# Token transforms of a spectral filter, split by even and odd frequency into quarters and halves of the TensorE array

## The chip, the cores and the metric

The kernel runs on one core of one Trainium2 chip. The metric is the time of one execution on the device in microseconds (us). Before the change the median of three runs is 439.57 us (439.55 to 439.62). One further execution was recorded by the profiler; durations, starts and waits below come from it.

## The reference, cut to what matters

```
xn  = layernorm(x)                                    # x: 2048 tokens x 448 channels
A   = irfft2(rfft2(xn) * (w_r + 1j * w_i))            # over tokens and channels, 225 channel frequencies
B   = (relu(xn @ W_gate) * (xn @ W_up)) @ W_down      # 448 -> 1792 -> 448
out = x + A + B
```

Everything is float32. The kernel writes each operand as a sum of two float16 parts, a high one and a low one, and multiplies high by high, high by low and low by high: three TensorE passes stand for one float32 product.

## The kernel before, in words

**Two streams of work share the engines.** The foreground is the gated network B: 56 gate units (14 slices of the hidden width times 4 chunks of tokens), each 40 passes of 512 columns on TensorE (some of them half passes over 64 rows), and three groups of down projections. After a gate unit ScalarE takes the relu (`gu_relu`, L966), VectorE multiplies by the up half (`gu_times`, L970, called the gate product below), ScalarE writes the high part (`gu_hi`, L974) and VectorE the low part (`gu_lo`, L978). Two PSUM buffers `gu` hold gate units, so the next but one unit can start when the gate product has read its buffer.

The background is the spectral branch A. A token number is 16 n1 + n2 and a token frequency is k1 + 128 k2. So the forward transform is, for each of 16 values n2, a channel transform (`f_dft`, for the pair n2 and n2 + 8), an eight-point butterfly on VectorE (`f_a`, `f_b`), the two float16 parts (`f_hi`, `f_lo`) and a transform over 128 tokens n1 (`f_sdft`), then a sixteen-point butterfly over n2. The spectrum is multiplied by the filter, and the inverse goes back the same way: `i_join` (last butterfly), `i_swap` (DMAs that bring cosine and sine rows to each other's partitions), `i_pair` (their sum), `i_mix` (an eight-point butterfly in two halves), `i_hi` on ScalarE and `i_lo` on VectorE, the token transform `i_sdft`, its two float16 parts `i_pqhi` (ScalarE) and `i_pqlo` (VectorE), and the channel transform `i_ddft`, which adds into the output. The inverse goes through p = 0 to 7, each p standing for the pair p and p + 8.

In `f_sdft` the stationary operand is a 128x128 matrix of cosines and sines and the moving one has 464 columns: three passes for each n2. In `i_sdft` the data stand still and the matrix moves: four blocks of 128, three passes of 128 columns each. Both use the whole array. `f_dft` and `i_ddft` use its two halves of 64 rows side by side. Their results and those of the token transforms go to two PSUM banks named `fx`.

**What sets the order.** The foreground units are emitted in a fixed sequence. Behind each, a planner takes background steps off a list. Each step carries a cost in VectorE time, and a share `load` of a unit's time, found by bisection, says how much background fits behind a unit, so that the list ends nine gate units before the end. A scheduler then puts the instructions into a fixed order for each engine; an engine takes its own in that order and waits on semaphores. `f_dft` and `i_ddft` are "offered": if half passes of a gate unit come by they are placed behind these, and every later matmul that is emitted is tied behind them (`state["bar"]`).

Of the kernel before, what the change touches and what calls it, by code (L numbers as in the profile page):

```python
# [20 lines left out]
NG = 8  # L21
# [23 lines left out]
SQ = 2.0 ** -16  # L45

# [29 lines left out]

def _freqs():


    p = np.arange(128)  # L80
    k1 = np.where(p < 64, p, np.where(p == 64, 64, 64 - p))
    return (k1[None, :] + 128 * np.arange(16)[:, None]) % S


def _constants():
# [54 lines left out]
    c_fm = c_fm.reshape(4, 4, 128, 2, 128).transpose(1, 2, 0, 3, 4)  # L140
# [6 lines left out]
def tile_gfnet_reglu(ctx: ExitStack, tc: tile.TileContext, x, xr, wgu, wd, wf, ident, c_fd, c_fm, c_im, c_row, c_id,  # L147
# [35 lines left out]

    eps = mt([128, 1], F32, "eps")
# [21 lines left out]
    state = {}  # L206
# [45 lines left out]
    def load_fm(q):  # L252
        t = ft([128, 4, 2, 128], F16, "fm", 4)
        nc.sync.dma_start(t, c_fm[q])
        for j in range(4):
            fm_t[q + 4 * j] = t[:, j]
# [155 lines left out]
    Fq, Xh, yps, cur = {}, {}, {}, {}  # L412
# [235 lines left out]
    def swap(key):  # L648
# [4 lines left out]
        nc.sync.dma_start(t[1:64], cur[key][65:128])  # L653
        nc.sync.dma_start(t[65:128], cur[key][1:64])
# [9 lines left out]
    def row_in(j):  # L664
        for par in range(2):
            nc.sync.dma_start(row[j + 8 * par:j + 8 * par + 1], cur["s1", j, par][64:65])

    def row_wf():
# [5 lines left out]
        for i in range(4):  # L674
            nc.sync.dma_start(w[32 * i:32 * i + 16], wf[:, 64, i // 2])
# [63 lines left out]
    def i_swap(p):  # L739
        u = U[p]  # L740
        for i in range(2):
            nc.sync.dma_start(u[64:65, :, :, KC * i:KC * (i + 1)], row[p + 8 * i:p + 8 * i + 1])
        t = sw[p] = state["sw"][p % 2]
        nc.sync.dma_start(t[1:64], u[65:128])
        nc.sync.dma_start(t[65:128], u[1:64])
# [26 lines left out]
    def i_sdft(n2):  # L772
        ps = fx()
        v, m = state["vt"][:, :, n2 // 8].rearrange("p a g k -> p a (g k)"), im_t[n2]
        for g in range(4):
            o = ps[:, 128 * g:128 * (g + 1)]
            for i, (h, c) in enumerate(((0, 0), (0, 1), (1, 0))):
                mm(o, v[:, h, 128 * g:128 * (g + 1)], m[:, c, :], start=(g + i == 0), stop=(i == 2),
                         skip_group_check=True)
        sps[n2] = ps  # L780

    def i_pqhi(n2):
        pgh[n2] = it([128, 1024], F16, "wf", 6).rearrange("p (a k) -> p a k", a=2)
        A.activation(pgh[n2][:, 0], sps[n2], AF.Copy, scale=2.0 ** -14)  # L784

    def i_pqlo(n2):
        V.scalar_tensor_tensor(pgh[n2][:, 1], sps[n2], 2.0 ** -14, pgh[n2][:, 0], op0=OP.mult, op1=OP.subtract)  # L787
# [259 lines left out]
    PE_US = {"f_dft": 0.85, "f_sdft": 0.59, "i_sdft": 0.65, "i_ddft": 0.82, "row_dft": 0.2}  # L1047
# [40 lines left out]
    add(0.0, f_dft, 0, 8)  # L1088
    for k, a in enumerate(seq):
# [14 lines left out]
        if k < 7:  # L1104
            add(0.0, force, f_dft, seq[k + 1], seq[k + 1] + 8)
        for n2 in (a, a + 8):
            add(0.0, f_sdft, n2)
# [84 lines left out]
    both(0.6, i_pqlo, 7)  # L1192
# [252 lines left out]
def _arrays(A_x, A_w_r, A_w_i, B_W_gate, B_W_up, B_W_down):  # L1445
# [39 lines left out]
```

## Time and profile before

| what | value |
|---|---|
| median of three runs | 439.57 us |
| profiled execution, first to last instruction | 438.4 us |
| TensorE (PE) busy | 430.9 us, 98% |
| VectorE (DVE) busy | 371.2 us, 85% |
| ScalarE (ACT) busy | 256.8 us, 59% |
| GpSimd (POOL) busy | 36.4 us, 8% |
| mean granted TensorE clock | 1.000 |

The profiled execution's own time is its span; no other time of it is given, and the median of the runs is 1.2 us above. A matmul's listed duration contains its way through the pipeline, so the pace of a block of matmuls is read from the starts of its first and of the next block. The same holds for VectorE, where the next instruction starts before the listed end of the last. "Idle before" in square brackets names what an engine waited for.

### The profile page before, as it was taken

The numbers are of one execution on the slowest core, as the hardware profiler recorded it, in microseconds if no ns is written. First come the engines' busy times: TensorE is split into PE (matmuls) and PEld (weight loads), VectorE is DVE, ScalarE is ACT, GpSimd is POOL, SyncE is SP. The second block draws the span as 40 slices with busy tenths as digits, with TensorE's granted clock in tenths as the row PEclk, the third lists the DMA queues.
The fourth block names the chain that finished last, engine by engine and source line by source line (L and its number), as shares of the span: only waits on it lengthen the run. The fifth ranks groups of instructions, "written<-read, shape, count | busy, mean of one in ns | idle before, by whom it ended". The sixth has DMA issues, their size and how long they took to land.

```text
span 438.4 us, 8109 instructions
## 1 busy us (share of the span) xinstructions
PE 430.9 (98%) x3014; PEld 209.9 (48%) x3014; DVE 371.2 (85%) x916; ACT 256.8 (59%) x519; POOL 36.4 (8%) x72
## 2 busy tenths in 40 slices
PE   6999999999999999999999999999999999999997
PEld 2644544454444444444444444444554555554544
DVE  5998798999967999899999999698989978976213
ACT  5897494486357856625413675574565665756620
POOL 1140040033300040000000011000000000000000
PEclk9999999999999999999999999999999999999999
DMA  8769992042000363530402100020111121301112
GB/s 261 253 164 304 384 236 65 2 80 31 3 0 2 133 198 119 163 120 24 144 13 86 43 1 1 2 81 7 55 45 53 47 67 56 119 24 50 43 42 84
DMA packets 37720, 39.53 MB, mean 90 GB/s; under 512 B 17952, under 2 KB 32576, under 8 KB 37680
## 3 DMA queue, kind: packets, MB, share of 16 engines
q1 hardware_dynamic: 37680, 39.01, 29.3%
q8 instruction: 23, 0.38, 0.4%
q14 instruction: 17, 0.14, 0.1%
HBM read 24.25 MB, written 3.67 MB: 64 GB/s over the span
## 4 chain that ended last, share of the span: by engine, by line
PE 97%; ACT 1%; DMA 1%; DVE 0%; issue 0%; SPq 0%
PE gu L450 59%; PE dn L450 27%; PE fx L450 7%; PE dn L1034 1%; PE gu L1034 1%; DMA y<-in_xr 1%; ACT tt L330 1%; ACT junk L192 0%; PE fx L406 0%; PE fx L1034 0%; ACT y L321 0%; DVE bst L265 0%; ACT rs L282 0%; PE gu L384 0%; DVE xy L1013 0%
## 5 line engine op out<-in xcount | busy, mean ns | idle before, releaser
L450 PE MATMUL gu<-T,wt 128*128 128x512 f16 (+2 forms) x1250 | 269.6, 376 | 0.0
L450 PEld LDWEIGHTS <-wt 128*128 128x128 f16 (+1 forms) x1250 | 111.7, 97 | 141.4 <-issue 19.9
L450 PE MATMUL dn<-wdt,h 128*128 128x448 f16 x624 | 126.8, 353 | 0.0
L450 PEld LDWEIGHTS <-h 128*128 128x128 f16 x624 | 60.2, 98 | 57.3 <-issue 0.4
L974 ACT ACTIVATE h<-g 128x512 f16<-128x512 f32 x56 | 35.1, 626 | 61.4 <-DVE g L970 61.3
L970 DVE SCALAR_TENSOR_TENSOR g<-gu,g 128x512 f32<-128x512 f32 x56 | 38.5, 687 | 21.0 <-ACT g L966 20.9
L966 ACT ACTIVATE g<-gu 128x512 f32<-128x512 f32 x56 | 33.0, 590 | 35.4 <-PE gu L450 35.4
L1006 ACT ACTIVATE xy<-dn,dsc 128x448 f32<-128x448 f32 x44 | 27.6, 627 | 28.0 <-PE dn L450 27.9
L978 DVE TENSOR_TENSOR h<-g,h 128x512 f16<-128x512 f32 x56 | 38.4, 687 | 5.5 <-ACT h L974 5.5
L995 ACT ACTIVATE dn<-xy,dinv 128x448 f32<-128x448 f32 x44 | 27.8, 632 | 0.6
L195 POOL PARTITION_ALL_REDUCE wm<-wm x15 | 13.8, 929 | 170.5 <-ACT junk L192 170.5
L866 DVE SCALAR_TENSOR_TENSOR wt<-wst,wsc,wt 128x512 f16<-128x512 f32 x28 | 20.4, 747 | 3.8 <-ACT wt L862 3.8
L862 ACT ACTIVATE wt<-wst,wsc 128x512 f16<-128x512 f32 x28 | 19.2, 715 | 1.0 <-DVE wsc L202 0.9
L787 DVE SCALAR_TENSOR_TENSOR wf<-fx,wf 128x512 f16<-128x512 f32 x16 | 10.8, 690 | 8.9 <-ACT wf L784 8.9
L192 ACT ACTIVATE junk<-wst 128x512 bf16<-128x512 f32 x28 | 17.4, 623 | 1.3 <-DMA wst<-in_wgu 1.1
L784 ACT ACTIVATE wf<-fx 128x512 f16<-128x512 f32 x16 | 9.5, 597 | 9.8 <-PE fx L450 9.2
L814 ACT ACTIVATE xy<-fx,fsc 128x448 f32<-128x448 f32 x16 | 9.2, 629 | 9.4 <-PE fx L450 9.4
L527 DVE TENSOR_TENSOR y<-y,y 128x464 f32<-128x464 f32 x21 | 13.4, 639 | 0.2
L528 DVE TENSOR_TENSOR y<-y,y 128x464 f32<-128x464 f32 x21 | 13.4, 637 | 0.0
L265 DVE BATCH_NORM_STATS2 bst<-y 128x6 f32<-128x448 f32 x16 | 9.3, 621 | 4.4 <-DMA y<-in_xr 4.4
L770 DVE SCALAR_TENSOR_TENSOR vt<-wst,fsc,vt 128x464 f16<-128x464 f32 x16 | 10.5, 701 | 2.9 <-ACT vt L765 2.9
L450 PEld LDWEIGHTS <-vt 128*128 128x128 f16 x192 | 11.5, 98 | 1.9
(159 smaller groups left out, 489.5 us busy)
## 6 DMA issues: line engine op xcount, KB each, us to landing
wst<-in_wgu SPq DMA_DIRECT2D x28, 256.0 KB
wf<-in_wf SPq DMA_DIRECT2D x16, 232.0 KB
sw<-y SPq DMA_DIRECT2D x32, 114.2 KB
sw<-wst SPq DMA_DIRECT2D x16, 228.4 KB
y<-in_xr SPq DMA_DIRECT2D x16, 224.0 KB
xy<-in_x SPq DMA_DIRECT2D x16, 224.0 KB
out<-xy SPq DMA_DIRECT2D x15, 224.0 KB
wdst<-in_wd SPq DMA_DIRECT2D x14, 224.0 KB
```

The source lines that it names most:

```text
L192: A.activation(mt([128, 512], BF16, "junk")[:, 0:src.shape[-1]], src, AF.Square, scale=SQ, accum_out=acc)
L195: G.partition_all_reduce(o, i, 128, bass_isa.ReduceOp.add)
L450: r = P.matmul(*a, **k)
L527: V.tensor_tensor(t, a, b, op=OP.add)
L862: A.activation(w[:, 0:4, :], wst[f, g], AF.Copy, scale=wsc[f, g])
L866: V.scalar_tensor_tensor(w[:, 4:8, :], st, sc, w[:, 0:4, :], op0=OP.mult, op1=OP.subtract)
L966: last["A"] = A.activation(g1s[f, q], hps[f, q][:, 0, :], AF.Relu, scale=2.0 ** -22).ins
L970: last["V"] = V.scalar_tensor_tensor(g1, hps[f, q][:, 1, :], 2.0 ** -22, g1, op0=OP.mult, op1=OP.mult).ins
L974: A.activation(ht[f, q][:, 0, :], g1s[f, q], AF.Copy)
L978: V.tensor_tensor(h[:, 1, :], g1s.pop((f, q)), h[:, 0, :], op=OP.subtract)
L995: A.activation(dps[n2][:, 0:D], xy[n2], AF.Copy, scale=dinv[:, g:g + 1])
L1006: last["A"] = A.activation(xy[n2], dps[n2][:, 0:D], AF.Copy, scale=dsc[:, g:g + 1]).ins
```

## The change: what it does

The 128 frequency rows are sorted anew, even frequencies on partitions 0 to 63 and odd ones on 64 to 127 (`_k1`), and the tokens of a chunk so that partitions p and p + 64 hold tokens 1024 apart (`_tokens`). For an even frequency the two token halves then enter as a sum, for an odd one as a difference, and each needs a transform over 64 tokens only.

Forward: `f_dft` leaves the second n2 of a pair in PSUM, ScalarE copies the first, and the new `f_fold` makes sum and difference on VectorE, two instructions that read PSUM. `f_sdft` runs once for a pair as 12 passes of 464 columns, each in one of four 64x64 quarters of the array. Inverse: `i_sdft` runs once for a pair as 48 passes of 64 columns, each in one half of 64 rows; the new `i_part` (ScalarE) and `i_unfold` (VectorE, two instructions that read PSUM) make sum and difference; `i_pqhi` becomes one instruction of 1024 elements, and `i_pqlo` reads SBUF where it read PSUM. The two `fx` banks become one tile. A swap is four DMAs where it was two; the matrices of the inverse come in 8 loads where they came in 16.

```diff
+PAIRS = ((slice(1, 32), slice(33, 64)), (slice(33, 64), slice(1, 32)), (slice(64, 96), slice(96, 128)),
+         (slice(96, 128), slice(64, 96)))
...
+    fx2 = psum.tile([128, 2, 512], F32, name="fx", bufs=1)
...
+        t = fa[a] = free.pop(0)
+        with tc.high_priority(offset=400):
+            A.activation(t.rearrange("p (i s) c k -> p i (s c k)", i=2), fx2[:, :, 0:4 * GW], AF.Copy,
+                         scale=2.0 ** -14)
+        return m
+
+    def f_fold(a):
+
         F = Fq[a] = ft([128, NG, 2, 2 * KC], F32, "eo", 2)
...
+        for b in range(2):
+            ps = fx2[:, :, 4 * GW:8 * GW].rearrange("p i (x k) -> p i x k", k=KC)
+            V.scalar_tensor_tensor(F[:, b], ps, (-1.0) ** b * 2.0 ** -14, t, op0=OP.mult, op1=OP.add)
+        free.append(fa.pop(a))
...
+    def f_sdft(a):
+        m, w = None, fm_t[a]
+        for k in range(2):
+            yps[a + 8 * k] = fx2[:, k, 0:XW].rearrange("p (g c k) -> p g c k", g=NG, c=2)
+        for i, (x, y) in enumerate(((0, 0), (0, 1), (1, 0))):
+            for k in range(2):
+                for b in range(2):
+                    p, q = slice(64 * k, 64 * k + 64), slice(64 * b, 64 * b + 64)
+                    xh = Xh[a + 8 * b].rearrange("p a g k -> p a (g k)")
+                    with tc.high_priority(offset=0 if m is None else 2000):
+                        m = chained(mm(fx2[q, k, 0:XW], w[p, b, x], xh[p, y], start=(i == 0), stop=(i == 2),
+                                       skip_group_check=True).ins, m)
...
+        for o, i in PAIRS:
+            nc.sync.dma_start(t[o], cur[key][i])
...
+    def i_sdft(p):
+        m = None
+        for b in range(2):
+            v, w = state["vt"][:, :, b].rearrange("p a g k -> p a (g k)"), im_t[p][:, b]
+            for g in range(4):
+                o = slice(64 * (2 * g + b), 64 * (2 * g + b + 1))
+                for i, (h, c) in enumerate(((0, 0), (0, 1), (1, 0))):
+                    for e in range(2):
+                        q = slice(64 * e, 64 * e + 64)
+                        with tc.high_priority(offset=0 if m is None else 2000):
+                            m = chained(mm(fx2[:, e, o], v[q, h, 128 * g:128 * (g + 1)], w[q, c],
+                                           start=(b + g + i == 0), stop=(i == 2), skip_group_check=True).ins, m)
+        return m
+
+    def i_part(p):
+        yu[p] = it([128, 2, 512], F32, "yu", 1)
+        A.activation(yu[p][:, 1], fx2[:, 0], AF.Copy, scale=2.0 ** -14)
+
+    def i_unfold(p):
+        y = yu[p]
+        for b in range(2):
+            V.scalar_tensor_tensor(y[:, b], fx2[:, 1], (-1.0) ** b * 2.0 ** -14, y[:, 1], op0=OP.mult, op1=OP.add)
+
+    def i_pqhi(p):
+        t = it([128, 2, 1024], F16, "wf", 3).rearrange("p x (h k) -> p x h k", h=2)
+        pgh[p], pgh[p + 8] = t[:, :, 0], t[:, :, 1]
+        A.activation(t[:, 0], yu[p], AF.Copy)
+
+    def i_pqlo(p):
+        y = yu.pop(p)
+        for b in range(2):
+            V.tensor_tensor(pgh[p + 8 * b][:, 1], y[:, b], pgh[p + 8 * b][:, 0], op=OP.subtract)
...
-    PE_US = {"f_dft": 0.85, "f_sdft": 0.59, "i_sdft": 0.65, "i_ddft": 0.82, "row_dft": 0.2}
+    PE_US = {"f_dft": 0.85, "f_sdft": 0.75, "i_sdft": 0.85, "i_ddft": 0.82, "row_dft": 0.2}
...
+        if k < 7:
+            add(0.0, force, f_dft, seq[k + 1], seq[k + 1] + 8)
+            add(1.27, f_fold, seq[k + 1])
         for n2 in (a, a + 8):
             add(0.54, f_lo, a, n2)
...
-        both(0.0, i_sdft, p)
-        both(0.0, i_pqhi, p)
+        add(0.0, i_sdft, p)
+        add(0.0, i_part, p)
         if p < 7:
             add(1.1, i_pair, p + 1)
+        add(1.3, i_unfold, p)
+        add(0.0, i_pqhi, p)
+        if p < 7:
             add(1.99, i_mix, p + 1, 0)
```

**How the order changes on TensorE.** The place is the inverse, from the end of `i_ddft` for p = 3 (operand `wf`) over `i_sdft` for p = 4 (`vt`) to `i_ddft` for p = 4 (`wf` again), with gate units `gu` and down projections `dn` around them. Before:

```order
L450 MATMUL fx_4467<-idc_t_84,wf_4348 128x56
L450 LDWEIGHTS wt_3462
L450 MATMUL gu_4580<-T1_64,wt_3462 128x512 [waits DVE_49]
...
L450 MATMUL dn_4744<-wdt_3716,h_4219 128x448
L450 LDWEIGHTS vt_2350 [waits DMAHW6_49,Activation_49]
L450 MATMUL fx_4521<-im_4202,vt_2350 128x128 [waits Activation_49]
...
L450 LDWEIGHTS wt_3560
L450 MATMUL gu_4601<-T1_64,wt_3560 128x512 [waits DVE_49]
...
L450 MATMUL dn_4746<-wdt_3713,h_4177 128x448
L450 LDWEIGHTS wf_4547 [waits Activation_49]
L450 MATMUL fx_4645<-idc_t_84,wf_4547 128x56 [waits Activation_49]
```

Now:

```order
L470 MATMUL gu_4739<-T1_65,wt_3534 128x512
L470 LDWEIGHTS wf_4445 [waits Activation_49]
L470 MATMUL fx_61<-idc_t_85,wf_4445 128x56 [waits Activation_49]
...
L470 LDWEIGHTS vt_2412 [waits Activation_49]
L470 MATMUL fx_61<-im_4287,vt_2412 128x64 [waits DMAHW6_49]
...
L470 LDWEIGHTS vt_2412 [waits DVE_49]
...
L470 LDWEIGHTS wf_4653 [waits DVE_49,Activation_49]
L470 MATMUL fx_61<-idc_t_85,wf_4653 128x56 [waits Activation_49]
...
L470 LDWEIGHTS wt_3580
L470 MATMUL gu_4760<-T1_65,wt_3580 128x512
```

Before, 20 full passes of a gate unit and two passes of `dn` stand between the first and the second spectral block, and half passes, 20 full passes and seven passes of `dn` between the second and the third. Now the three spectral blocks (48 passes each) follow each other with nothing between, directly behind the last half pass of gate unit `gu_4739`, and gate unit `gu_4760` stands behind all three.

**The order on VectorE at the same place, now.** From the gate product of `gu_4739` (L1021) to the low part that the third block needs (L838, `i_pqlo` for p = 4); L450, L451, L460 and L461 are the end of `i_mix`, L549 to L770 belong to `i_join`, L805 is `i_lo`, L696 and L697 are `i_pair`, L828 is `i_unfold`, L438 to L443 the next `i_mix`; where a row's mate of the same shape follows, it is left out:

```order
L1021 SCALAR_TENSOR_TENSOR g1_4888<-gu_4739,g1_4888 128x512 [waits Activation_49]
L450 TENSOR_TENSOR wst_4101<-wst_4101 128x2x58 [waits DVE_49]
...
L460 SCALAR_TENSOR_TENSOR wst_4101<-wst_4447 128x2x116 [waits DVE_49]
...
L549 SCALAR_TENSOR_TENSOR y16_83<-y2_69 128x8x29
...
L1029 TENSOR_TENSOR h_4891<-g1_4888,h_4891 128x512 [waits Activation_49]
L769 SCALAR_TENSOR_TENSOR wst_4520<-y16_83,y14_81 128x16x29 [waits DVE_49]
...
L805 SCALAR_TENSOR_TENSOR vt_2412<-wst_4101,fsc_89,vt_2412 128x16x29 [waits Activation_49]
...
L696 TENSOR_TENSOR wst_4300<-wst_4300,sw1_2415 128x8x58 [waits DMAHW3_49,DMAHW4_49,DMAHW2_49,DMAHW7_49,DMAHW1_49,DMAHW0_49]
...
L828 SCALAR_TENSOR_TENSOR yu_4647<-fx_61,yu_4647 128x512 [waits Activation_49]
...
L438 TENSOR_TENSOR wst_4655<-wst_4300 128x2x232
...
L442 TENSOR_TENSOR wst_4300<-wst_4655 128x3x116 [waits DVE_49]
...
L838 TENSOR_TENSOR wf_4653<-yu_4647,wf_4653 128x512 [waits Activation_49]
```

All of it stands behind the gate product, which itself reads what TensorE finishes just before the first of the three blocks.

More of the change, by code (lines that the diff above doesn't have):

```diff
@@ L74, in _fd_parts, with _tokens, _k1 @@
     return {n: GW * i for i, n in enumerate(names)}, GW * 8
+def _tokens():
+    b, p = np.arange(16)[None, :], np.arange(128)[:, None]
+    return (1024 * (b // 8) + 16 * (p % 64) + b % 8 + 8 * (p // 64)).reshape(-1)
+def _k1():
+    i, odd = np.arange(128) % 32, np.arange(128) // 64
+    sine = np.arange(128) // 32 % 2
+    k1 = 2 * i + odd
+    k1[ROW], sine[ROW] = 64, 0
+    return k1, sine.astype(bool)
 def _freqs():
-    p = np.arange(128)
-    k1 = np.where(p < 64, p, np.where(p == 64, 64, 64 - p))
-    return (k1[None, :] + 128 * np.arange(16)[:, None]) % S
+    k1, sine = _k1()
+    return (np.where(sine, -k1, k1)[None, :] + 128 * np.arange(16)[:, None]) % S
 def _constants():
@@ L182, in tile_gfnet_reglu @@
     dinv = mt([128, len(GROUPS)], F32, "dinv")
+    state = {}
     eps = mt([128, 1], F32, "eps")
@@ L252, in load_fm @@
     def load_fm(q):
-        t = ft([128, 4, 2, 128], F16, "fm", 4)
+        t = ft([128, 2, 2, 2, 64], F16, "fm", 4)
         nc.sync.dma_start(t, c_fm[q])
-        for j in range(4):
+        for j in range(2):
             fm_t[q + 4 * j] = t[:, j]
@@ L599, in open_inv @@
         for t in state["sw"]:
-            for p in (0, 64):
+            for p in (0, ROW):
                 G.memset(t[p:p + 1], 0.0)
@@ L665, in row_in @@
         for par in range(2):
-            nc.sync.dma_start(row[j + 8 * par:j + 8 * par + 1], cur["s1", j, par][64:65])
+            nc.sync.dma_start(row[j + 8 * par:j + 8 * par + 1], cur["s1", j, par][ROW:ROW + 1])
     def row_wf():
@@ L741, in i_swap @@
         for i in range(2):
-            nc.sync.dma_start(u[64:65, :, :, KC * i:KC * (i + 1)], row[p + 8 * i:p + 8 * i + 1])
+            nc.sync.dma_start(u[ROW:ROW + 1, :, :, KC * i:KC * (i + 1)], row[p + 8 * i:p + 8 * i + 1])
         t = sw[p] = state["sw"][p % 2]
-        nc.sync.dma_start(t[1:64], u[65:128])
-        nc.sync.dma_start(t[65:128], u[1:64])
+        for o, i in PAIRS:
+            nc.sync.dma_start(t[o], u[i])
     def i_pair(p):
@@ L770, in i_lo @@
             V.scalar_tensor_tensor(lo[:, b], u[:, b], fsc[:, 0:1], hi[:, b], op0=OP.mult, op1=OP.subtract)
[L772 to L787, printed above, removed]
+    def i_sdft(p):
[10 more added lines that the diff above has]
+                                           start=(b + g + i == 0), stop=(i == 2), skip_group_check=True).ins, m)
+        return m
+    def i_part(p):
[13 more added lines that the diff above has]
+            V.tensor_tensor(pgh[p + 8 * b][:, 1], y[:, b], pgh[p + 8 * b][:, 0], op=OP.subtract)
     ips, late = {}, set()
@@ L1088, in tile_gfnet_reglu @@
     add(0.0, f_dft, 0, 8)
+    add(1.27, f_fold, 0)
     for k, a in enumerate(seq):
@@ L1101, in tile_gfnet_reglu @@
             add(0.0, f_hi, a, n2)
+        if k < 7:
+            add(0.0, force, f_dft, seq[k + 1], seq[k + 1] + 8)
+            add(1.27, f_fold, seq[k + 1])
         for n2 in (a, a + 8):
             add(0.54, f_lo, a, n2)
[L1104 to L1107, printed above, removed]
+        add(0.0, f_sdft, a)
         for fn, q in extra.get(k, ()):
@@ L1170, in tile_gfnet_reglu @@
     bring(1)
-    both(0.0, load_im, 0)
+    add(0.0, load_im, 0)
     add(1.1, i_pair, 0)
@@ L1175, in tile_gfnet_reglu @@
         if p:
-            both(0.6, i_pqlo, p - 1)
+            add(1.2, i_pqlo, p - 1)
             add(0.0, offer, i_ddft, p - 1, p + 7)
         if p < 7:
-            both(0.0, load_im, p + 1)
+            add(0.0, load_im, p + 1)
         add(2.14, i_mix, p, 1)
@@ L1186, in tile_gfnet_reglu @@
             add(0.0, force, i_ddft, p - 1, p + 7)
-        both(0.0, i_sdft, p)
-        both(0.0, i_pqhi, p)
+        add(0.0, i_sdft, p)
+        add(0.0, i_part, p)
         if p < 7:
             add(1.1, i_pair, p + 1)
+        add(1.3, i_unfold, p)
+        add(0.0, i_pqhi, p)
+        if p < 7:
             add(1.99, i_mix, p + 1, 0)
-    both(0.6, i_pqlo, 7)
+    add(1.2, i_pqlo, 7)
     add(0.0, i_ddft, 7, 15)
```

68 lines of the change are left out of this document (29 added, 39 removed).

## The prediction

> **What bounds the kernel now.** I read the page first, then the table by stage, then the order of time.
>
> ```profile
> span 438.4 us, 8109 instructions
> PE 430.9 (98%) x3014; PEld 209.9 (48%) x3014; DVE 371.2 (85%) x916; ACT 256.8 (59%) x519; POOL 36.4 (8%) x72
> PE 97%; ACT 1%; DMA 1%; DVE 0%; issue 0%; SPq 0%
> 80.00:120.00 40.00, 40.00 (x330) 19.30 (x328) 39.44 (x109) 25.24 (x54) 11.37 (x15) 1.00 0.20 32
> 200.00:240.00 40.00, 40.00 (x199) 18.23 (x198) 39.61 (x90) 14.71 (x34) 0.00 (x0) 1.00 0.20 64
> 240.00:280.00 40.00, 40.00 (x201) 18.66 (x199) 38.44 (x98) 22.88 (x53) 3.67 (x4) 1.00 0.06 21
> 360.00:400.00 40.00, 40.00 (x381) 21.27 (x380) 34.06 (x79) 24.46 (x41) 0.00 (x0) 1.00 0.17 56
> ```
>
> The chain that ended last is TensorE for 97% of the span, and in every stage shown it is busy 40.00 of 40 us: a microsecond less of matmul issue is a microsecond less of time, as long as no operand comes late. VectorE (third number in a stage) is close behind: 39.4 and 39.6 of 40 us in two stages, and never late so far. So the change takes work off the engine that bounds and puts some on the one with least room. Three things have to be priced: the passes saved, the room on VectorE, and whether the new order makes TensorE wait.
>
> **The passes.** Starts in the order of time give the pace of whole blocks:
>
> ```profile
> 86.80 1.34 PE L450 MATMUL fx<-Xh,fm 128*128 128x464 f16 x6
> 87.98 2.11 PE L450 MATMUL gu<-T,wt 128*128 128x512 f16 x9
> 340.94 1.50 PE L450 MATMUL fx<-im,vt 128*128 128x128 f16 x24
> 342.28 3.00 PE L450 MATMUL dn<-wdt,h 128*128 128x448 f16 x15
> 345.30 3.83 PE L450 MATMUL gu<-T,wt 128*128 128x512 f16 x17
> 349.07 0.79 PE L450 MATMUL fx<-idc_t,wf 64*128 64x56 f16 x48
> 349.80 4.52 PE L450 MATMUL dn<-wdt,h 128*128 128x448 f16 x23
> 61.43 4.32 PE gu L450 x20
> 13.79 1.38 PE L406 MATMUL fx<-id_t,tt 128*64 128x128 f16 x24
> 15.10 0.50 PE L450 MATMUL gu<-T,wt 128*128 128x256 f16 x3
> ```
>
> A pair in `f_sdft` takes 87.98 - 86.80 = 1.18 us (6 passes, 0.196 each); a pair in `i_sdft` 342.28 - 340.94 = 1.34. A block of 48 half-array passes of 56 columns takes 349.80 - 349.07 = 0.73. The 17 full passes ahead of it took 3.77 where 17 x 0.216 (4.32 / 20) is 3.67: coming into a block of another tile shape costs 0.10.
>
> `i_sdft` becomes 48 half-array passes of 64 columns: 0.73 x 64/56 = 0.83, less the part that does not grow, plus 0.10 for the shape: 0.92. Saved 0.42 for each p, 3.4 us for eight. Bounds: 0.83 in all (saves 4.1) and 1.10 (saves 1.9).
>
> `f_sdft` becomes 12 passes of 464 columns in four quarters. If four run side by side it is three rounds of 0.196, 0.59, plus 0.10, and something for twelve weight loads: I take 0.75. Saved 0.43, 3.4 us for eight. The trace has no quarters. Its nearest row speaks against them: the 24 passes over column halves (L406) took (15.10 - 13.79) / 24 = 0.055 us each, what a pass of 128 columns takes alone (1.34 / 24 = 0.056), so two column halves did not overlap there. By that row the twelve passes would take 6 x 0.196 + 0.10 = 1.28 (only row halves overlap) or 12 x 0.196 + 0.10 = 2.45 (none do): bounds from 3.9 saved to 10.2 lost. I stay with 0.75, since loading 24 separate weights in 1.31 us could set that pace as well, and would then cost 0.66 for twelve. [...]
>
> **Room on VectorE.** These rows, in order of time, price its instructions by the distance from start to start:
>
> ```profile
> 361.64 1.31 DVE L770 SCALAR_TENSOR_TENSOR vt<-wst,fsc,vt 128x464 f16<-128x464 f32 x2
> 362.15 0.79 PE L450 MATMUL fx<-idc_t,wf 64*128 64x56 f16 x48
> 362.87 0.64 DVE L661 TENSOR_TENSOR wst<-wst,sw 128x464 f32<-128x464 f32 x1
> 363.04 1.16 ACT L814 ACTIVATE xy<-fx,fsc 128x448 f32<-128x448 f32 x2 [0.94 <-PE fx L450]
> 363.27 0.76 SPq L745 DMA_DIRECT2D sw<-wst  x1
> 365.17 0.63 DVE L418 TENSOR_TENSOR wst<-wst 128x464 f32<-128x464 f32 x1
> 365.29 0.63 ACT L974 ACTIVATE h<-g 128x512 f16<-128x512 f32 x1 [1.10 <-DVE g L970]
> 365.72 0.64 DVE L420 TENSOR_TENSOR wst<-wst 128x464 f32<-128x464 f32 x1
> 366.87 0.52 DVE L422 TENSOR_TENSOR wst<-wst 128x348 f32<-128x348 f32 x1
> 367.31 0.52 DVE L423 TENSOR_TENSOR wst<-wst 128x348 f32<-128x348 f32 x1
> 369.08 1.36 DVE L787 SCALAR_TENSOR_TENSOR wf<-fx,wf 128x512 f16<-128x512 f32 x2 [1.25 <-ACT wf L784]
> 370.36 0.27 DVE L435 TENSOR_TENSOR wst<-wst 128x116 f32<-128x116 f32 x1
> 370.38 0.58 ACT L966 ACTIVATE g<-gu 128x512 f32<-128x512 f32 x1
> 371.49 0.68 DVE L970 SCALAR_TENSOR_TENSOR g<-gu,g 128x512 f32<-128x512 f32 x1
> 372.09 0.27 DVE L430 TENSOR_TENSOR wst<-wst 128x116 f32<-128x116 f32 x1
> 372.28 0.27 DVE L431 TENSOR_TENSOR wst<-wst 128x116 f32<-128x116 f32 x1
> 372.90 0.39 DVE L441 SCALAR_TENSOR_TENSOR wst<-wst 128x232 f32<-128x232 f32 x1
> 373.21 0.40 DVE L515 SCALAR_TENSOR_TENSOR y<-y 128x232 f32<-128x232 f32 x1
> 373.33 1.10 ACT L765 ACTIVATE vt<-wst,fsc 128x928 f16<-128x928 f32 x1 [0.49 <-DVE wst L441]
> ```
>
> 464 elements cost 0.55 (365.72 - 365.17), 512 0.60 (372.09 - 371.49), two with PSUM as source 1.28 (370.36 - 369.08), 348 0.44, 232 0.31, 116 0.19. `f_fold` is 16 instructions of 464 from PSUM, some 16 x 0.56 = 9.0 us; `i_unfold` 16 of 512, 16 x 0.62 = 9.9; `i_pqlo` loses a little (0.62 to 0.60, -0.3). Together 18.6 us more VectorE work in a stretch where the stages above leave 0.4 to 6 us in 40. The planner answers by packing denser: worked out from its own list of costs, its share goes from 0.92 to 1.00. Nothing goes under nothing here: less than no wait isn't possible, and if VectorE falls behind by more than the two `gu` buffers cover, TensorE waits. The idle time between 80 and 400 us is some 28 us by such stages, so most of the 18.6 fits; I take 1.5 us of waits, bounds 0 and 4. ScalarE loses 8 evictions forward and gains 8 copies inverse at 59% busy: nothing. The 48 more swap DMAs cost SyncE about 0.8 us each to issue (L745: 0.76), and the sums that need them (`i_pair`) come a whole p later, some 12 us: nothing, and 1.6 us per p if that cover were gone.
>
> **The wait that the order builds.** The order shown above puts three spectral blocks behind each other and a gate unit behind all three. TensorE takes them in that order, so while the second waits for `i_lo` (p = 4) and the third for `i_pqlo`, 20 full passes and the down projections stand behind, though ready. Until now such passes covered this chain: the block at 362.15 is followed by 20 of them. The chain starts at the gate product of `gu_4739`, which cannot start before the last half pass ahead of the blocks has ended. From there (t = 0):
>
> - relu: starts 0.2 after the matmul (0.94 idle and 0.89 from block start to eviction at 363.04, where the block takes 0.72), takes 0.58 (L966): 0.8. Gate product 0.60: 1.4.
> - 2 x 0.19 + 2 x 0.31 + 2 x 0.31 (end of `i_mix`, start of `i_join`) = 1.6: 3.0. Low part of the gate 0.60: 3.6. Two of 464: 1.1: 4.7. `i_hi` (1.10 on ScalarE, L765) lies inside.
> - `i_lo`, two in 362.87 - 361.64 = 1.23: 6.0. Last half of `i_sdft`, 0.4: 6.4. Without waiting TensorE would be there at 0.82 + 0.92 = 1.7: **first wait 4.7 us**.
> - `i_part` 0.2 + 0.6: 7.2. `i_unfold` 1.24: 8.4. Then ScalarE writes a seed (0.6) and `i_pqhi` (1.10 x 1024/928 = 1.2): 10.2; VectorE does 2 x 0.55 + 2 x 0.44 of the next `i_mix` meanwhile: 10.4. `i_pqlo` 1.2: 11.6. Last half of `i_ddft` 0.4: 12.0. Without the second wait that block would end 0.73 after 6.4: **second wait 4.9 us**.
>
> Together 9.6 us. It can't be much less, since each step is in an engine's fixed order behind the one before: with no latencies between engines and ScalarE never busy elsewhere, 8.0. If VectorE comes to it late by two microseconds, 12. I looked for a second such place: the other spectral blocks, forward and inverse, keep at least two passes of foreground before and mostly 4 us behind them.
>
> **Sum.** 438.4 - 3.4 - 3.4 + 9.6 + 1.5 = 442.7 us of span. The median of the runs lies 439.57 - 438.4 = 1.2 above its profiled span: **443.9 us**, 1.0% slower. The saving is real, and one place in the order gives back more than all of it.
>
> **Rivals.**
>
> 1. *Quarters don't overlap.* For it: L406. Against it: the half-array blocks overlap (48 passes of 56 columns in 0.73 us is 0.015 each, less than the 0.056 x 56/128 = 0.024 of one alone). With row halves alone the term is +0.8 instead of -3.4: 448.1. With no overlap +10.2, and VectorE then gets its room back: 456.0.
> 2. *The clock falls during the wait.* TensorE stands still twice for over 4 us. The first passes of the program are the only ones behind such a pause:
>
> ```profile
> 1.88 5.31 PE L1294 MATMUL dn<-bw 128*128 128x512 f16 x16 [1.88 <-POOL bw L1366]
> ```
>
>    Less the 0.48 of the last one's listed length, 15 steps in 4.83 us: 0.32 each, where 0.216 is the pace later: 1.6 us lost. Twice that is 3.2: 447.1. Against it: a few small passes fall inside each pause, and the granted clock reads 1.00 even in that opening, so the column won't tell. [...]
> 3. *The gain outweighs the wait.* `f_sdft` and `i_sdft` run at bare pace with no price for the change of shape (0.59 and 0.73: 4.7 + 4.9 = 9.6 saved), the wait is at its floor of 8.0 and VectorE holds: 436.8 of span, 438.0, faster by 0.4%. It decides as soon as what the blocks save passes the wait. For it: every term is within its bounds; against it: the 0.10 at the block's entry is in the trace, and the floor leaves out the latencies that the rows show.
> 4. *VectorE is late all along.* Its term is 4 instead of 1.5 and the chain starts late: 448.0. For it: 39.6 of 40 us already. Against it: between 360 and 400 us 6 of 40 are free.
>
> **How the numbers follow.** Forecast 0.50, rival 1 0.12 (three parts in four with row halves), rival 2 0.14, rival 3 0.15, rival 4 0.09. The measurement tells 0.2% from no change, 0.9 us. Rival 3 gives 0.12 to faster and 0.03 to the same; the forecast gives another 0.05 to the same (wait 8, savings at their best); the rest, 0.80, is slower. The likeliest case's own range is 441 to 446.5; with the rivals, leaving out the outer edges of 1 and 3, 437 to 449.
>
> **What would show it.** Right: the table of waits, which has no line of TensorE waiting for VectorE now, gets two in the `fx` blocks on L470, for L805 and L838, of over 4 us each, at one place some 350 us into the span; around it ScalarE and VectorE work while TensorE's row is empty. Twelve quarter passes from start to next block near 0.75, 48 passes of 64 columns near 0.85. VectorE's busy time near 390 us. Wrong: if TensorE stands busy through that place; if a quarter block takes 1.28 or 2.45; if the passes after the pause run at 0.3 or 0.4 us instead of 0.216 (then rival 2); if waits on L1021 spread over the middle stages add up to several microseconds (then rival 4).

## The result, and the profile after

The changed kernel takes 489.18 us (487.87 to 490.31, four runs) against 439.6 us before: a ratio of 1.1126, 95% interval 1.1101 to 1.1151. The prediction had the direction and the wait in the inverse; the time lies 45 us above its 443.9 and 40 above the upper end of its range.

From the page of the changed kernel: span, busy times, the granted clock in 40 slices, the chain that ended last, and three groups (busy, mean ns, idle time before them and its releaser).

```profile
span 486.1 us, 8687 instructions
PE 437.3 (90%) x3254; PEld 204.9 (42%) x3254; DVE 392.5 (81%) x952; ACT 253.3 (52%) x508; POOL 28.9 (6%) x72
PEclk9999999999999999869899968997999998799999
PE 46%; DVE 29%; DMA 14%; ACT 5%; issue 4%; SPq 2%; DVEq 0%; ACTq 0%
L470 PE MATMUL gu<-T,wt 128*128 128x512 f16 (+2 forms) x1250 | 277.3, 384 | 30.9 <-DVE g L1021 30.9
L696 DVE TENSOR_TENSOR y<-y,sw 128x232 f32<-128x232 f32 x16 | 6.4, 398 | 29.1 <-DMA sw<-y 22.8
L648 ACT ACTIVATE wf<-wf 128x116 f32<-128x116 f32 x16 | 4.5, 295 | 21.0 <-DMA wf<-in_wf 21.0
```

TensorE was 97% of the chain before and is 46% of it now. A new releaser has appeared, DMA with 14%: transfers into `sw`, the tile that a swap fills. The table by stage (TensorE busy, weight loads, VectorE, ScalarE, GpSimd, granted clock, DMA share, GB/s) shows where:

```profile
200.00:240.00 40.00, 27.96 (x119) 11.46 (x117) 27.17 (x62) 11.88 (x27) 0.00 (x0) 0.83 0.23 61
280.00:320.00 40.00, 30.55 (x137) 13.42 (x137) 34.97 (x90) 21.06 (x48) 2.35 (x5) 0.83 0.05 13
320.00:360.00 40.00, 31.99 (x238) 14.32 (x237) 31.39 (x78) 16.33 (x32) 0.43 (x1) 0.91 0.13 38
400.00:440.00 40.00, 30.67 (x406) 16.26 (x405) 33.95 (x79) 22.45 (x35) 0.00 (x0) 0.87 0.17 54
```

TensorE stands still 8 to 12 us in each of four stages that were full before, and its granted clock falls there, to 0.83 to 0.91 in the mean of a stage. Only the last of them is the place that the prediction named. In the first one VectorE is busy 27 us where it was 39.6: it isn't overloaded, it waits too. The chain of waits in that stage, in order of time:

```profile
187.94 8.63 DMA sw<-y
...
196.59 9.79 DMA sw<-y
```

These are the swaps of the filter stage (`swap`, 16 of them, between the forward transform and the multiplication by the filter). A piece of the chain is a transfer from issue to landing, and the swap ahead of it is still under way in it. The pace is that of the sums that wait for the swaps (L696):

```profile
192.12 0.40 DVE L696 TENSOR_TENSOR y<-y,sw 128x232 f32<-128x232 f32 x1 [2.85 <-DMA sw<-y]
197.15 0.40 DVE L696 TENSOR_TENSOR y<-y,sw 128x232 f32<-128x232 f32 x1 [2.21 <-DMA sw<-y]
202.06 0.40 DVE L696 TENSOR_TENSOR y<-y,sw 128x232 f32<-128x232 f32 x1 [2.50 <-DMA sw<-y]
206.95 0.40 DVE L696 TENSOR_TENSOR y<-y,sw 128x232 f32<-128x232 f32 x1 [3.01 <-DMA sw<-y]
```

A swap lands every 4.9 to 5.0 us; in the kernel before, four such sums started within 4.6 us, from 177.94 to 182.57. VectorE takes its work in order, so a sum that waits for a swap (L696) holds up the gate product (L1021) behind it, and this holds TensorE: behind the sum of 206.95 the gate product starts at 208.20, and TensorE goes on at 208.94 after 8.15 us of waiting for it. Such waits are the 30.9 us of the `gu` line.

### The profile page after: what moved, and what is told of

The parts are those of the page before. It is cut to its first block, busy times and chain, and to the rows that moved or that the text cites. A ratio compares the mean times of both kernels' runs of the same rounds, so it can differ in the third digit from the quotient of the medians.

```text
span 486.1 us, 8687 instructions
## 1 busy us (share of the span) xinstructions
PE 437.3 (90%) x3254; PEld 204.9 (42%) x3254; DVE 392.5 (81%) x952; ACT 253.3 (52%) x508; POOL 28.9 (6%) x72
## 4 chain that ended last, share of the span: by engine, by line
PE 46%; DVE 29%; DMA 14%; ACT 5%; issue 4%; SPq 2%; DVEq 0%; ACTq 0%
PE gu L470 27%; PE dn L470 12%; DMA sw<-y 12%; PE fx L470 4%; DVE h L1029 2%; DVE g L1021 2%; DVE wt L917 2%; SPq L689 2%; ACT junk L213 2%; DVE y L561 1%; DVE y L656 1%; DVE y L562 1%; DVE y L577 1%; DVE y L659 1%; DVE y L576 1%
## 5 line engine op out<-in xcount | busy, mean ns | idle before, releaser
L470 PE MATMUL gu<-T,wt 128*128 128x512 f16 (+2 forms) x1250 | 277.3, 384 | 30.9 <-DVE g L1021 30.9
L470 PEld LDWEIGHTS <-wt 128*128 128x128 f16 (+1 forms) x1250 | 113.2, 99 | 172.9 <-issue 57.2
L470 PE MATMUL dn<-wdt,h 128*128 128x448 f16 x624 | 129.3, 355 | 0.8 <-ACT dn L1046 0.4
L1021 DVE SCALAR_TENSOR_TENSOR g<-gu,g 128x512 f32<-128x512 f32 x56 | 38.2, 683 | 17.8 <-ACT g L1017 17.7
L696 DVE TENSOR_TENSOR y<-y,sw 128x232 f32<-128x232 f32 x16 | 6.4, 398 | 29.1 <-DMA sw<-y 22.8
L216 POOL PARTITION_ALL_REDUCE wm<-wm x15 | 7.5, 498 | 186.2 <-ACT junk L213 186.2
L800 ACT ACTIVATE vt<-wst,fsc 128x928 f16<-128x928 f32 x8 | 8.8, 1102 | 14.3 <-DVE wst L461 14.3
L648 ACT ACTIVATE wf<-wf 128x116 f32<-128x116 f32 x16 | 4.5, 295 | 21.0 <-DMA wf<-in_wf 21.0
L828 DVE SCALAR_TENSOR_TENSOR yu<-fx,yu 128x512 f32<-128x512 f32 x16 | 11.0, 688 | 2.0 <-ACT yu L823 1.6
L805 DVE SCALAR_TENSOR_TENSOR vt<-wst,fsc,vt 128x464 f16<-128x464 f32 x16 | 10.5, 699 | 2.3 <-ACT vt L800 2.3
```

The source lines that it names most:

```text
L470: r = P.matmul(*a, **k)
L1021: last["V"] = V.scalar_tensor_tensor(g1, hps[f, q][:, 1, :], 2.0 ** -22, g1, op0=OP.mult, op1=OP.mult).ins
```

## The experiments

Three causes were on the table. **A**: the pieces of 31 rows themselves; the change cuts a swap of twice 63 rows into 31, 31, 32 and 32. **B**: four transfers a swap instead of two on SyncE's queue. **C**: the pool of `wf` buffers, or VectorE's greater load. For what is left after that, **D**: VectorE's load, and **E**: the order of the work.

One remark on what some kernels compute. In the changed kernel and those made from it, `i_ddft` for p = 6 meets tokens whose down projection is still open, and their sums stay in `fx` until `i_acc` (L881) fetches them; for block 14 that comes after `i_sdft` for p = 7 has written the same tile (458.34 us against 455.40 in the trace of the changed kernel), so its spectral part is replaced. In `e7_pool_lo`, `e8_pool_lo_early` and `e10_early` more of the output is wrong; which part, no row shows. No instruction is left out by it.

### Pieces of 32 rows in the changed kernel

```diff
-PAIRS = ((slice(1, 32), slice(33, 64)), (slice(33, 64), slice(1, 32)), ...
+PAIRS = ((slice(0, 32), slice(32, 64)), (slice(32, 64), slice(0, 32)), ...
```

> The changed kernel with one edit: the two swap pieces of 31 rows are 32 rows long (rows 0 and 32 come along, and their sums, which should stay as they are, get a wrong addend; nothing else is left out). The order of every engine and the number of transfers are as in the changed kernel, 489.2 us. Theory A, the 31 rows themselves: a piece of 31 rows takes some 8 us to land because it is not spread over the DMA engines, and VectorE stands behind it. Then the 22.8 us and 8.3 us of VectorE waiting for swaps fall under 5 us together, the 30.9 us of TensorE waiting for L1021 nearly go, the one wait in the inverse (9.2 us) stays, and the time is 441 to 449 us. Theory B, four transfers a swap instead of two fill SyncE's queue: no change, 485 us or more. Theory C, the pool of wf buffers or VectorE's load: no change either, 480 us or more.

Measured: 452.64 us, ratio to before 1.0294 (1.0279 to 1.0310). One row more in half of the transfers takes 36.5 of the 49.6 us away. From its table of waits (in all, times, longest, in us):

```profile
PE gu L470 <- DVE g L1021: 4.1, 5, 1.3
DVE wst L696 <- DMA sw<-wst: 1.7, 1, 1.7
```

and from its chain that ended last (start, length):

```profile
194.81 2.09 DMA sw<-y
...
207.50 2.01 DMA sw<-y
```

The waits of VectorE for swaps of `y`, 22.8 us, are no longer listed; TensorE waits 4.1 us for L1021 instead of 30.9, and where the chain still passes through a swap it takes 2 us (once 3.3), not 8 to 10. A holds. The number of transfers, the pool and VectorE's work are as in the changed kernel, so B and C make at most what is left. (ScalarE's wait of 21.0 us for `wf`, which speaks for C in the page of the changed kernel, decides nothing: with 16 and 15 rows, further below, it is 24.7 us in a kernel that is 31 us faster.) The time is 4 us above the upper end that A gave, which the sections below take up.

### The same cut in the kernel before

```diff
-        nc.sync.dma_start(t[1:64], cur[key][65:128])
-        nc.sync.dma_start(t[65:128], cur[key][1:64])
+        for o, i in PAIRS:
+            nc.sync.dma_start(t[o], cur[key][i])
+PAIRS = [... for a, n in ((1, 31), (65, 31), (32, 32), (96, 32))]
```

> The kernel before with one edit: each swap is cut into four pieces of 31, 31, 32 and 32 rows, as the change cuts it, instead of two of 63. Theory A: the 31-row pieces alone bring the stalls of the middle stages, 455 to 485 us. Theory B: slower as well, 455 to 485 us. Theory C: within 1 us of 439.6.

The other cut has `((1, 48), (65, 48), (49, 15), (113, 15))` in place of these numbers:

> The kernel before with each swap cut into four pieces as well, but of 48, 48, 15 and 15 rows. Theory A: 48 and 15 rows spread over the DMA engines, so 439 to 441 us. Theory B (the count of transfers): as slow as the cut into 31 and 32, 455 to 485 us. Theory C: within 1 us of 439.6.

Measured: 465.93 us with 31 and 32 rows (ratio 1.0597, 1.0579 to 1.0614), 439.44 us with 48 and 15 (0.9997, 0.9987 to 1.0006). Four transfers a swap cost nothing by themselves; pieces of 31 rows cost 26 us in a kernel that is otherwise the old one. From the chain of the first, with 31 and 32 rows:

```profile
186.52 8.43 DMA sw<-y
...
207.33 8.70 DMA sw<-y
```

With 48 and 15 rows the chain's shares on the page are those of before:

```profile
PE 97%; ACT 1%; DVE 1%; DMA 1%; issue 0%
```

### What it is about 31

63 and 15 rows are odd too, and fast. The table by stage tells more: first the kernel before while swaps of 63 rows follow each other, then the changed kernel while pieces of 31 rows are under way (the last two numbers are the mean busy share of the 16 DMA engines and GB/s):

```profile
178.00:182.00 4.00, 4.00 (x23) 2.06 (x21) 4.00 (x10) 2.65 (x6) 0.00 (x0) 1.00 0.45 145
196.00:198.00 2.00, 2.00 (x11) 0.93 (x10) 0.85 (x3) 0.00 (x0) 0.00 (x0) 1.00 0.07 25
```

0.45 of 16 is 7.2 engines in the mean, 0.07 is 1.1: pieces of 31 rows keep about one engine busy at a time. Two tests: 62 rows, one less than 63 and even, in the kernel before, and 16 + 15 rows, the same rows in shorter pieces, in the changed kernel.

```diff
+PAIRS = [... for a, n in ((1, 62), (65, 62), (63, 1), (127, 1))]
```

> The kernel before with each swap cut into pieces of 62, 62, 1 and 1 rows. The cut into 31 and 32 rows gave 465.9 us, the cut into 48 and 15 gave 439.4. [...]

```diff
+PAIRS = ((slice(1, 17), slice(33, 49)), (slice(17, 32), slice(49, 64)), (slice(33, 49), slice(1, 17)), (slice(49, 64), slice(17, 32)), ...
```

> The changed kernel (489.2 us) with the two pieces of 31 rows cut into 16 and 15 rows: six transfers a swap instead of four, 144 instead of 96 in all, and the same rows as in the changed kernel. [...] If SyncE's issue time is the next bound: 455 to 470 us. If pieces of 31 rows were slow only as two transfers that follow each other in the same rows, 480 us or more.

Measured: 468.16 us with 62 rows (1.0650, 1.0634 to 1.0666), so an odd length is not the cause; 458.02 us with 16 and 15 rows in the changed kernel (1.0421, 1.0406 to 1.0437). From the chain with 62 rows:

```profile
185.61 9.21 DMA sw<-y
...
226.08 9.77 DMA sw<-y
```

From the table by stage of the kernel before with 31 and 32 rows, and then with 62:

```profile
189.00:192.00 3.00, 0.27 (x2) 0.02 (x1) 1.71 (x5) 0.00 (x0) 0.00 (x0) 1.00 0.07 25
189.00:192.00 3.00, 0.34 (x2) 0.09 (x1) 1.84 (x6) 0.00 (x0) 0.00 (x0) 1.00 0.13 50
```

0.07 and 0.13 of 16 are 1.1 and 2.1 engines, at 25 GB/s each. At that rate a row of 1856 bytes takes 0.074 us and 62 rows take 4.6 us (estimates from these rows), which is nearly the whole pace of the swaps, 4.9 to 5.0 us. So 62 rows over two engines take as long as twice 31 over one: each engine has 62 rows for a swap either way. A piece of 48 rows lands 2.3 us after its issue (the median on the page of the kernel with 48 and 15 rows), where 48 rows on one engine would make 3.6 us (an estimate at the same rate), so more than one carries it. From 62 rows to 63 the mean number of engines at work goes from 2.1 to 7.2; by what rule, and which engines they are, no row shows.

With 16 and 15 rows the landing is quick again (where the chain passes through a swap it takes 0.8 to 2.0 us), but six transfers a swap bring SyncE in. Its issues (SPq) are 4% of the chain on that kernel's page, 2% on that of the changed one and 1% with pieces of 32 rows:

```profile
PE 47%; DVE 33%; ACT 7%; SPq 4%; DMA 4%; issue 3%; POOL 0%; DVEq 0%; ACTq 0%
```

The time is 5.4 us above that with pieces of 32. So B is nothing at four transfers and, as far as the chain shows it, a few microseconds at six.

### The wait in the inverse

In the kernel with pieces of 32 rows the place stands free of other trouble. Starts on TensorE in order of time:

```profile
367.81 0.78 PE L470 MATMUL fx<-idc_t,wf 64*128 64x56 f16 x48
371.78 0.29 PE L470 MATMUL fx<-im,vt 64*128 64x64 f16 x4 [3.19 <-ACT vt L800]
373.59 1.35 PE L470 MATMUL fx<-im,vt 64*128 64x64 f16 x44 [1.52 <-DVE vt L805]
379.32 0.28 PE L470 MATMUL fx<-idc_t,wf 64*128 64x56 f16 x4 [4.38 <-ACT fx L849]
379.78 1.25 PE L470 MATMUL fx<-idc_t,wf 64*128 64x56 f16 x44 [0.18 <-DVE wf L838]
380.96 6.52 PE L470 MATMUL gu<-T,wt 128*128 128x512 f16 x20
387.32 0.92 PE L470 MATMUL dn<-wdt,h 128*128 128x448 f16 x4
```

and the table by stage of the same kernel in steps of 4 us (the clock is the third number from the end):

```profile
368.00:372.00 4.00, 0.81 (x50) 0.61 (x42) 3.97 (x12) 3.38 (x5) 0.00 (x0) 0.93 0.00 0
372.00:376.00 4.00, 1.42 (x48) 1.19 (x44) 3.63 (x7) 0.60 (x1) 0.00 (x0) 0.50 0.28 62
376.00:380.00 4.00, 0.50 (x14) 0.45 (x16) 3.93 (x8) 2.14 (x3) 0.00 (x0) 0.50 0.33 76
380.00:384.00 4.00, 4.00 (x52) 2.00 (x46) 3.90 (x15) 2.26 (x3) 0.00 (x0) 0.50 0.22 81
384.00:388.00 4.00, 4.00 (x18) 1.65 (x16) 2.88 (x6) 0.48 (x1) 0.00 (x0) 0.86 0.45 115
```

The two waits are 3.19 + 1.52 = 4.7 us and 4.38 + 0.18 = 4.6 us, 9.3 together. Then the price of the clock: it is granted at 0.50 in three whole steps, 12 us, and in part of the next. The 20 gate passes take 387.32 - 380.96 = 6.36 us where 4.32 is their pace, and the two blocks of 44 passes take about 0.5 us more each than in other places: 3.1 us. The next kernel takes the wait away by the order, together with a mask that keeps rows 0 and 32 as they should be:

```diff
-        state["job"] = (state["at"], fn, a, 6.0)
+        state["job"] = (state["at"], fn, a, 10.0 if fn is i_ddft else 6.0)
...
-        V.tensor_tensor(u[:, :, 0], u[:, :, 0], t[:, :, 1], op=o1)
-        V.tensor_tensor(u[:, :, 1], u[:, :, 1], t[:, :, 0], op=o2)
+        for c in range(2):
+            m = state["mask"][:, (c + (sgn < 0)) % 2:][:, 0:1]
+            V.scalar_tensor_tensor(u[:, :, c], t[:, :, 1 - c], m, u[:, :, c], op0=OP.mult, op1=OP.add)
```

> The changed kernel with swap pieces of 32 rows, the two rows that must not change masked by a factor of 0 per row in the sums (the same number of VectorE instructions of the same size), and the inverse transform's i_ddft put into the foreground passes 10 us after it is offered instead of 6, which in the order leaves foreground passes between all spectral blocks of the inverse. If the wait of 9.2 us comes from the three blocks behind each other, it goes, and with theory A the time is 438.4 - 3.7 (f_sdft at 0.72) - 4.2 (i_sdft at 0.81) + 0 to 3 + 1.2 = 432 to 435 us, faster than both. If the wait only moves elsewhere, 440 to 446 us. With theory B or C 470 us or more.

Measured: 442.12 us, ratio to before 1.0060 (1.0040 to 1.0080). The wait is gone and the time falls by 10.5 us. It isn't the 432 to 435 us of the expectation, nor faster than before. It lies in the 440 to 446 that stood for a wait that only moves, but the listed waits fell, from 9.3 + 4.1 us to 5.7. What TensorE still waits for, after its start (starts, in brackets the idle time; the profiled execution took 441.15 us, the shortest of six):

```profile
154.73 4.48 PE L470 MATMUL gu<-T,wt 128*128 128x512 f16 x20 [1.08 <-DVE g L1023]
...
296.23 5.03 PE L470 MATMUL gu<-T,wt 64*128 64x512 f16 x24 [2.85 <-DVE g L1023]
...
434.78 1.31 PE L1087 MATMUL fx<-wdt,h 128*128 128x224 f16 x12 [1.11 <-ACT xy L867]
```

With two smaller ones (0.43 and 0.26) they come to 5.7 us. The last stems from the new order, which moves the last `i_ddft` among the last down projections.

### VectorE's load, or the order

The first test moves the low parts `f_lo` and `i_pqlo`, 32 subtractions, to GpSimd, costs them at nothing in the list, and ends the list two units earlier (LASTGU 11); the second ends it one more unit earlier (LASTGU 12).

```diff
-        V.tensor_tensor(Xh[n2][:, 1], f_part(a, n2), Xh[n2][:, 0], op=OP.subtract)
+        G.tensor_tensor(Xh[n2][:, 1], f_part(a, n2), Xh[n2][:, 0], op=OP.subtract)
```

> The kernel e4_rows32_spread (442.1 us) with 32 subtractions moved from VectorE to GpSimd (f_lo and i_pqlo, some 18 us of VectorE), costed at nothing in the background list, and the background told to end two gate units earlier. In e4 TensorE still stands idle 5.7 us after its start: 1.1, 0.4, 0.3 and 2.9 us behind VectorE and 1.1 us behind ScalarE near the end. Theory D, VectorE's load makes these waits: with its 18 us given back they nearly go, and the time is 434 to 438 us, faster than before. Theory E, the order of the work makes them, or GpSimd is too slow or slows VectorE: 440 us or more.

> e7_pool_lo with the background told to end one more gate unit earlier, so that the last i_ddft stands ahead of four down projections in the order instead of inside the last two, but two spectral blocks of the inverse stand behind each other once. Theory D: 432 to 438 us, 1 us less than e7 at the end, and 0 to 4 us more where the two blocks meet. Theory E: 440 us or more.

Measured: 452.15 us and 460.71 us, slower than `e4_rows32_spread` by 10 and 19. They don't decide between D and E, since VectorE got nothing back. From the groups of the first, GpSimd's subtractions (busy, mean ns, idle before):

```profile
L840 POOL TENSOR_TENSOR wf<-yu,wf 128x512 f16<-128x512 f32 x16 | 21.0, 1334 | 116.5 <-ACT wf L835 88.6
L527 POOL TENSOR_TENSOR Xh<-eo,Xh 128x464 f16<-128x464 f32 x16 | 19.0, 1203 | 77.1 <-ACT Xh L524 63.6
```

from its groups with the shapes kept apart, an addition on VectorE that uses none of their data:

```profile
L455 DVE TENSOR_TENSOR wst<-wst 128x116 f32<-128x116 f32 x8 | 8.9, 1110 | 0.0
```

and the same addition without GpSimd beside it, in `e4_rows32_spread`:

```profile
L455 DVE TENSOR_TENSOR wst<-wst 128x116 f32<-128x116 f32 x8 | 2.2, 270 | 0.0
```

It takes 1.11 us instead of 0.27, and VectorE is busy 393.4 us with 32 instructions fewer (394.2 with them). So VectorE lost beside GpSimd what it was to gain; what holds the addition up there, no row shows.

So the test was made again with ScalarE, by copies of the same size in place of the low parts, with the list of costs of `e4_rows32_spread`:

```diff
-            V.tensor_tensor(pgh[p + 8 * b][:, 1], y[:, b], pgh[p + 8 * b][:, 0], op=OP.subtract)
+            A.activation(pgh[p + 8 * b][:, 1], y[:, b], AF.Copy, scale=2.0 ** -12)
```

> The kernel e4_rows32_spread (442.1 us) with the 32 subtractions f_lo and i_pqlo replaced by 32 copies of the same size on ScalarE (what is left out: the low parts of these spectral operands; the copies hold a scaled high part instead). [...] Theory D, VectorE's load makes what is left of the waits (5.7 us) and part of what else e4 loses: 433 to 438 us. Theory E, the order makes them: 440 us or more.

> The kernel e4_rows32_spread (442.1 us) with the background told to end three gate units earlier (LASTGU 12 instead of 9): the last i_ddft moves ahead of the last down projections, where e4 waited 1.1 us and moved a block of 0.7 us behind the last foreground work; two spectral blocks of the inverse meet once near the end; the list is packed denser by the planner. If the end of e4 is what costs, 439 to 441 us. If VectorE's load is (theory D), the denser list costs more than the end gives: 442 to 446 us.

Measured: 442.42 us (1.0054, 1.0034 to 1.0074) with VectorE at 376.6 instead of 394.2 us, and 450.36 us (1.0247, 1.0232 to 1.0262) with the denser list. From the kernel with copies on ScalarE, the wait that is left in the middle, in order of time:

```profile
295.62 6.48 PE L470 MATMUL gu<-T,wt 64*128 64x512 f16 x24 [2.54 <-DVE g L1023]
```

and the stage around it:

```profile
294.00:298.00 4.00, 2.38 (x8) 0.72 (x8) 3.97 (x8) 1.84 (x3) 1.14 (x1) 0.66 0.40 86
```

17.6 us less on VectorE change nothing in the time. The waits of 1.08 and 0.43 us go, but that of 2.54 stays, and the clock falls behind it (0.66). The subtractions that were replaced run at 57 to 168 and at 321 to 430 us in `e4_rows32_spread`, and this wait lies between the two. VectorE is as full around it as it was (3.97 of 4 us), with the weights' low parts (`w_lo`) and the first `i_join` ahead of a gate product. So the run speaks against a load that counts wherever it lies, and it leaves open whether load or order makes this wait.

The kernel that ends its list earlier lies above both ranges of its expectation. Its 8 us stand at one place near the end:

```profile
413.01 1.03 PE L470 MATMUL fx<-idc_t,wf 64*128 64x56 f16 x44 [1.31 <-DVE wf L840]
419.20 1.46 PE L470 MATMUL fx<-im,vt 64*128 64x64 f16 x48 [5.15 <-DVE xy L883]
...
429.22 1.10 PE L470 MATMUL dn<-wdt,h 128*128 128x448 f16 x5 [1.48 <-ACT dn L1048]
```

Here two spectral blocks stand behind each other, and the second, `i_sdft` for p = 7, waits 5.15 us until `i_acc` (L883) has fetched the sums of the first out of `fx`. The three waits make 7.9 us, and VectorE is busy for only 2.76 of the 4 us from 414 to 418, so most of this loss is the order, E, and not a denser packing of VectorE. For the waits of 1 to 3 us that `e4_rows32_spread` has left, the runs don't decide between D and E.

## Why the prediction was wrong, and where it was right

**The step that failed** stands in the part "Room on VectorE": "The 48 more swap DMAs cost SyncE about 0.8 us each to issue (L745: 0.76), and the sums that need them (`i_pair`) come a whole p later, some 12 us: nothing". It measured 36.5 us. Three things are wrong in it. It priced a transfer by its issue, and took for granted that the landing stays as it was; a piece of 31 rows lands 8 to 10 us after its issue instead of 2, and one swap follows the other at 4.9 to 5.0 us. It looked for cover in the inverse alone, where `i_pair` has it; 16 of the 24 swaps belong to the filter stage, where two follow each other in every round and their 10 us have no such cover. And it left out what VectorE's order makes of a late sum: the gate product behind it, TensorE, and then the clock. The price that it named for a lost cover, 1.6 us per p, is the issue time again.

**The wait that the order builds**: right, in its place and its two parts: 4.7 and 4.6 us where 4.7 and 4.9 were worked out (4.8 and 4.6 in the changed kernel). The sign named for it came only in part: L805 and L838 end 1.5 and 0.2 us of the two waits, and most is listed with ScalarE, 3.19 us for `i_hi` (L800) and 4.38 for the seed (L849), which the working has as earlier links of the same chain. It lies at 404 to 417 us in the changed kernel and at 368 to 381 with pieces of 32 rows, where some 350 was named.

**Rival 2, the clock**: right in size beside that wait, 3.1 us where 3.2 was given, though by luck in how it is made up: 1.6 behind each pause were priced, and 0.5, 0.5 and 2.0 were measured. It is wrong in saying that the column won't tell: the granted clock reads 0.50 in three steps of 4 us. With the forecast's other terms it was part of the truth and not an alternative to it. How long a pause brings the clock down, the runs don't settle: with pieces of 32 rows it fell at about 371.4 us (an estimate from the 0.93 of the step from 368 to 372 us and the 0.50 of the next), some 2.9 us after the last pass; behind the 2.54 us above it fell too (0.66 over 4 us), behind the 2.85 us of `e4_rows32_spread` it did not (1.00).

**The passes**: right in kind, and somewhat dearer than priced. In the changed kernel a quarter block and an inverse block, with the passes ahead of them and the start of the next block behind:

```profile
92.09 0.81 PE L470 MATMUL gu<-T,wt 128*128 128x512 f16 x3
92.83 0.78 PE L470 MATMUL fx<-Xh,fm 64*64 64x464 f16 x12
93.55 3.63 PE L470 MATMUL gu<-T,wt 128*128 128x512 f16 x16
...
422.29 0.92 PE L470 MATMUL dn<-wdt,h 128*128 128x448 f16 x4
423.14 0.87 PE L470 MATMUL fx<-im,vt 64*128 64x64 f16 x48
423.95 3.96 PE L470 MATMUL dn<-wdt,h 128*128 128x448 f16 x20
```

The blocks take 0.72 and 0.81 us. The entry comes on top, 0.1 as priced: the 3 gate passes ahead take 0.74 where 3 x 0.216 is 0.65, the 4 of `dn` 0.85 where 0.76 is their pace. The blocks before the change had no such entry (nine gate passes ahead of one took 130.86 - 128.92 = 1.94 us, 9 x 0.216). So a block costs 0.82 where 0.75 was taken, and 0.91 where 0.92 was. The last quarter block is cut into three pieces among down projections, which costs 0.6 us more (0.32, 0.32 and 0.51 us, and two entries). In all 8 x (1.18 - 0.82) + 8 x (1.34 - 0.91) - 0.6 = 5.7 us are saved, not 6.8. Rival 1 falls: the four quarters run side by side, 12 passes in 0.72 us where twelve one after another, at 0.196, would make 2.35.

**Room on VectorE**, the rest of it: VectorE's work grew by 392.5 - 371.2 = 21.3 us, where 18.6 was worked out. With pieces of 32 rows TensorE waits 4.1 us for L1021, just above the upper bound of 4, not 1.5.

**The sum again**, for the kernel with pieces of 32 rows, 13.0 us above before: - 5.7 for the blocks, + 9.3 for the wait, + 3.1 for the clock behind it, + 4.1 for L1021: 10.8. Some 2 us are not assigned. For `e4_rows32_spread`, 2.5 above before, - 5.7 for the blocks and + 5.7 for the waits leave 2.5 open; in its profiled execution, with a span 1.0 longer than before (439.4 against 438.4), it is 1.0. No matmul record is missing between these traces: each has 1102 full gate passes of 512 columns, 36 of 256, 112 half passes and 648 passes of the down projections' full form. (A gate unit has 20 full and 2 half passes in them, not the 40 of the description above.)

**Rival 3** was said to have every term within its bounds, but its savings of 4.7 and 4.9 lie beyond the 3.9 and 4.1 that the part on the passes gives as bounds. With 5.7 us saved it didn't come near.

**Rival 4** (VectorE late all along) has its sign in the trace, waits on L1021 over all middle stages, and the wrong cause: for the 30.9 us VectorE was not late by its load, it stood waiting for transfers. (By its own terms, 4 for 1.5 and 12 for 9.6, it would give 448.8, not 448.0.)

## What to carry to other kernels

When a transfer is cut, price its landing and not only its issue: look how long each piece is under way and how many engines it keeps busy (here 1.1 of 16 with 31 rows, 7.2 with 63). A piece with one row more and a mask on the receiving side can be cheaper than the exact piece: here the row more took 36.5 us away. And ask of each wait on an in-order engine what stands behind it: here a late swap reached TensorE through a gate product that had nothing to do with it.

## What the runs showed of the hardware

- A transfer of 31 or 62 rows of 1.8 KB holds the chain about 8 to 10 us, one of 32 rows about 2 (once 3.3). In the kernel before, cuts into 63 rows and into 48 and 15 took 439.6 and 439.44 us, into 31 and 32 and into 62 rows 465.93 and 468.16. While pieces of 31 and of 62 rows are under way, 25 and 50 GB/s flow and 1.1 and 2.1 of 16 DMA engines are busy (7.2 with 63 rows, at 145 GB/s), so a row takes its engine 0.074 us (an estimate from these rows).
- Two waits of 4.7 and 4.6 us with 48 small passes between them left TensorE at a granted clock of 0.50 for over 12 us, from some 2.9 us after the last pass (an estimate); behind a pause of 2.54 us the clock fell in one kernel (0.66 over 4 us), behind one of 2.85 us it did not in another (1.00).
- Going from passes over the whole array into a block over halves or quarters costs about 0.1 us at the block's entry (0.74 us for three gate passes that take 0.65 elsewhere, 0.85 for four of `dn` that take 0.76).
- GpSimd's subtractions of 464 and 512 elements took 1.20 and 1.33 us, and additions of 116 elements on VectorE beside them 1.11 instead of 0.27 us.
